# Attention, Fourier mixing and a feed-forward block on one core: a norm's tile, a weight block's step, closing folds, weight scales and a norm behind its halves are moved

## The chip, the cores and the metric

The kernel runs on one core of one Trainium2 chip. The metric is the device time of one execution in microseconds (us), the median of several runs. Five engines work side by side, each through its own queue in order: TensorE (PE: matmuls and transposes, with PEld for its weight loads), VectorE (DVE), ScalarE (ACT), GpSimd (POOL) and SyncE (SP), whose queue issues nearly all DMAs. An instruction waits at the head of its queue until what it needs is there, and everything behind it on that engine waits too.

## The reference, cut to what matters

```
# q, k, v: 8 batches, 12 heads, 448 tokens, 64 per head; w_ch1 768x3072; w_ch2 3072x768
attn = sigmoid(q @ k.T / sqrt(64) - log(448))        # per head, no softmax
x    = heads side by side of attn @ v                # 8 x 448 x 768
u    = x + real(fft(fft(x, axis=tokens), axis=768))  # mixing
un   = (u - mean(u)) / sqrt(var(u) + 1e-6)           # per token
out  = u + relu(un @ w_ch1) @ w_ch2
```

## The kernel before, in words

**Stages.** The 3584 tokens go through three stages: attention with mixing (0 to about 376 us in the profile), the first chunk of 512 tokens through the feed-forward block with plain products (about 384 to 592 us), and six further chunks with a seven-product scheme (to the end). Every matmul that needs more than half precision is made of a high and a low half.

**The step clock of the attention stage.** The loop at line 596 counts a step t from 0 to 202 by twos. Eight steps are one group of four heads (24 groups, 24 steps per batch). In each pass the program writes down scores (lines 139 to 160; ACT takes the sigmoid at line 133), then whatever was registered with `at(t, ...)` for steps t and t+1, then the products with v (line 183; ACT copies them to `xT`, line 192) or, in the third pass of a group, a piece of the mixing of the batch before (`mix_some`). `pin()` chains the instructions of each engine in the order in which they were written down, so an engine's queue order is the program's order.

**What is registered.** (1) `fold` (lines 196 to 217) forms sums and differences of `xT` rows in three levels, ending in the tile `xp`, from which the mixing's matmuls `psd` (line 237) read; the table FOLDS gives step, part and number. All folds are POOL's, except in the last batch, where those at steps after 27 with an odd number are DVE's. (2) `mix_units` (line 227): matmuls `psd`, copies `A` by ACT (line 241), matmuls `pss` (line 247), sums `sm`, `df` by DVE (line 256), transposes `psx` (line 268), sums `u` by DVE (line 277), and stores of `u` to `u_dram`. The tile `u` has four buffers; `psd`, `pss`, `psx` and the products with v share four PSUM banks. (3) `weight(n, step)` (line 308) takes one of 48 blocks of w_ch1 and w_ch2: step 0 loads it into one of four `wr` buffers (SP, line 315), step 1 is ACT's absolute value (line 326), step 2 DVE's maximum (line 331), step 3 three DVE operations that pack it (lines 335 to 340), step 4 its store (SP, line 343). The list `ends` (line 574) has the end step of each block, sorted, and the distances of its five steps from there. A block is named by its end step below: block 90 is the one that ends at step 90. (4) `weight_top`, `weight_row`, `weight_all` and `weight_scales` (lines 345 to 387) turn the 48 maxima into the scales `wsc` through one PE transpose and one small matmul. (5) `norm` (line 429) normalizes the first chunk, four row tiles i of 128 tokens: two loads, statistics, and for each i a cast to a high half by ACT (line 448, n = 8), the low half by DVE (line 452) and two transposing DMAs of the tile `hl` (line 454, n = 9). `hl` has one buffer.

**The first chunk.** `pair` (line 467) makes the feed-forward weights of one block pair: load `wq`, ACT scale (line 482), DVE low half (line 484), four POOL sums (line 492), ACT and DVE once more, store to `w_dram`. The loop at line 835 goes over f: for each f, steps of `pair` around the 18 matmuls of `up_proj` (line 636), then the steps of `fast_norm` that `norm_at` has for this f (the norm of the second chunk, in two halves tp of 18 steps: 0 loads `U`, 1 and 2 statistics, 3 to 6 the inverse root, 8 and 9 scale the rows, 10 to 12 transpose on PE, 13 to 17 sums and halves), then the 24 matmuls of `down_proj` (line 656), then `evac` (line 639), in which ACT and DVE empty the bank `psh` into `hh` and `hl`. `psh` and the transposes `pst` share two banks.

Of the kernel before, what the change touches and what calls it, by code (L numbers as in the profile page):

```python
# [8 lines left out]
F16 = mybir.dt.float16  # L9
F32 = mybir.dt.float32  # L10
# [13 lines left out]
DM = 768  # L24
# [18 lines left out]
NPLAIN = 1  # L43
# [12 lines left out]
def spectral_attention_ffn(tc, qk, v, w1, w2, cd, cs, ident_in, out):  # L56
    nc = tc.nc
    B = qk.shape[0]
# [6 lines left out]
    with ExitStack() as top:  # L65
# [20 lines left out]
        if True:  # L86
            c1 = mix.enter_context(tc.tile_pool(name="c1", bufs=1, side="right"))
            fx = mix.enter_context(tc.tile_pool(name="fx", bufs=1, side="right"))
# [107 lines left out]
            def fold(b, p, n, e):  # L196

                xT, xp, last = xts[b]
                if p == 0 and n == 0:
                    fds[b] = fx.tile([128, 2, 4, HS], F32, tag="fd", name="fd")  # L200
                fd = last if p == 2 else fds[b][:, p]
                lv, n = divmod(n, 2)
                op = (ALU.add, ALU.subtract)[n]
                if lv == 0:
                    if n == 0:
                        eos[p] = fx.tile([128, 2, 2, HS], F32, tag="eo", name="eo")
                    e.tensor_tensor(out=eos[p][:, n], in0=xT[:, p], in1=xT[:, p + 3], op=op)  # L207
                elif lv == 1:
                    eo = eos[p]
                    e.tensor_tensor(out=fd[:, 2 * n:2 * n + 2], in0=eo[:, :, 0], in1=eo[:, :, 1], op=op)  # L210
                elif lv == 2:
                    k = slice(1, 3) if n else slice(0, 4, 3)
                    e.tensor_tensor(out=fd[:, k], in0=fd[:, k], in1=fds[b][:, 1, k], op=op)
                else:
                    fd = fd.rearrange("p (c r) n -> p c r n", c=2)
                    e.tensor_tensor(
                        out=xp[:, n, :, :, 1 - p // 2], in0=fd[:, :, :, 0:HM], in1=fd[:, :, :, HS - 1:HM - 2:-1], op=op)

            def turn_rows(b, back):

                fd, tmp = fds[b], turn[b % 2]
                pairs = ((fd[64:65], tmp[1:3] if back else tmp[0:2]), (fd[0:1, 1:2], tmp[0:1] if back else tmp[2:3]))
                for x, y in pairs:
                    x, y = x.rearrange("o a k n -> o (a k n)"), y.rearrange("(o a) k n -> o (a k n)", o=1)
                    nc.gpsimd.dma_start(*((x, y) if back else (y, x)))
# [165 lines left out]
            def stats(c, j, u):  # L391
                stt = sm.tile([128, 2, 6], F32, tag="st", name="stt")
                for h in range(2):
                    nc.vector.bn_stats(out=stt[:, h], in_=u[:, h * 384:(h + 1) * 384])
                if j == 0:
                    mvs[c] = sm.tile([128, 8, 2], F32, tag="mv", name="mv")
                nc.vector.bn_aggr(out=mvs[c][:, 0:2, j], in_=stt)
# [25 lines left out]
            def scale_rows(c, j, u):  # L423
                mv = mvs[c]
                nc.vector.tensor_scalar(
                    out=u, in0=u, scalar1=mv[:, 0, j:j + 1], scalar2=mv[:, 3, j:j + 1],
                    op0=ALU.subtract, op1=ALU.mult)

            def norm(c, i, n, pool):
                if n == 0:  # L430
                    u = pool.tile([128, DM, 2], F32, tag="un", name="un")
                    u = u.rearrange("p n w -> p (n w)").rearrange("p (i n) -> p i n", i=2)
                    r0 = c * TW + i * 128
                    nc.sync.dma_start(u, u_dram[r0:r0 + 256, :].rearrange("(i p) n -> p i n", p=128))
                    uns[c, i], uns[c, i + 1] = u[:, 0], u[:, 1]
                elif n == 1:
                    stats(c, i % 2, uns[c, i])
                elif n < 6:
                    rsqrt(c, n, nc.vector if n == 2 else nc.gpsimd)
                elif n == 7:  # L440
                    scale_rows(c, i % 2, uns[c, i])
                elif n == 8:
                    u = uns[c, i]
                    if i == 0:
                        ut = ut0.tile([128, 2, NCC * TW], F16, name="ut0")
                        uts[c] = [ut[:, n].rearrange("p (m t) -> p m t", m=NCC) for n in range(2)]
                    hl = fx.tile([128, 2, DM], F16, tag="hl", name="hl")
                    nc.scalar.activation(hl[:, 0], u, AF.Copy)
                    uns[c, i] = u, hl
                else:  # L450
                    u, hl = uns.pop((c, i))
                    nc.vector.tensor_tensor(out=hl[:, 1], in0=u, in1=hl[:, 0], op=ALU.subtract)
                    for n in range(2):
                        nc.sync.dma_start(uts[c][n][:, :, i * 128:(i + 1) * 128], hl[:, n], transpose=True)
# [74 lines left out]
            def pin():  # L529

                ins = nc.cur_bb.bb.instructions
                for i in ins[seen[0]:]:
                    e = str(i.engine)
                    if e in seen[1]:
                        tc.add_manual_dep(
                            i, seen[1][e].name,
                            mybir.DependencyInfo(mybir.DependencyClass.NoSync, mybir.DependencyReason.DATA),
                            reason="order")
                    seen[1][e] = i
                seen[0] = len(ins)  # L540
# [10 lines left out]
            TP = TQ - 12  # L551
            extra = {}

            def at(t, fn):
                extra.setdefault(t, []).append(fn)

            for b in range(B):
                for t, p, n in FOLDS:
                    e = nc.vector if b == B - 1 and t > 27 and n % 2 else nc.gpsimd
                    at(24 * b + t, lambda b=b, p=p, n=n, e=e: fold(b, p, n, e))  # L560
                for k, t in enumerate((22, 25)):
                    at(24 * b + t, lambda b=b, k=k: turn_rows(b, k))
                at(24 * b + 34, lambda b=b: units.extend(mix_units(b)))
            for gg in range(1, GG):
# [3 lines left out]
                for w in range(2):  # L568
                    for n, fn in enumerate((cast, rest)):
# [1 line left out]
            at(17, lambda: nc.sync.dma_start(cd_sb, cd))  # L571
            at(22, lambda: (nc.sync.dma_start(cs_sb, cs), nc.sync.dma_start(ident, ident_in[:, 0]),
                            nc.sync.dma_start(perm, ident_in[:, 1:])))
            ends = sorted([(t, (-10, -5, -1, 0, 3)) for t in range(15, TP, 8)]
                          + [(t, (-11, -3, -1, 0, 3)) for t in range(17, TP, 8)]
                          + [(t, (-10, -2, -1, 0, 3)) for t in (34, 58, 82, 90, 130, 178)])
            for n, (t, ds) in enumerate(ends[:2 * NFC]):
                for step, d in enumerate(ds):
                    at(t + d, lambda n=n, step=step: weight(n, step))
            assert len(ends) >= 2 * NFC  # L580
            at(TP, weight_top)
            at(TP + 4, weight_row)
            at(TP + 6, weight_all)
            at(TP + 6, weight_scales)
            for p, d in ((0, 0), (1, 1)):
                for step, e in enumerate((0, 8 + p, 9 + p)):
                    at(TP + d + e, lambda p=p, step=step: pair(0, p, step))
# [33 lines left out]
        with ExitStack() as fast, ExitStack() as st:  # L621
# [3 lines left out]
            ps_h = fast.enter_context(tc.tile_pool(name="ps_h", bufs=2, space=PSUM))  # L625
# [13 lines left out]
            def evac(c, f):  # L639
                ps = hs[c, f]  # L640
                hh = up.tile([128, TW], F16, tag="hh", name="hh")
                hl = up.tile([128, TW], F16, tag="hl", name="hl")
                nc.scalar.activation(hh, ps, AF.Relu)
                nc.vector.scalar_tensor_tensor(  # L644
                    out=hl, in0=ps, scalar=0.0, in1=hh, op0=ALU.max, op1=ALU.subtract)
                hs[c, f] = (hh, hl)
# [60 lines left out]
            f, m = 1, 0  # L707
# [121 lines left out]

            norm_at = {}  # L830
            for tp in range(2):
                for f, steps in enumerate(((0,), (1,), (2,), (3, 4, 5), (6, 7), (8, 9), (10,), (11,), (12,),
                                           (13, 14), (15, 16), (17,))):
                    norm_at.setdefault(HELD + 1 + 11 * tp + f, []).extend((tp, n) for n in steps)
            for f in range(HELD + 1, NFC + HELD + 1):
                for n in range(2):
                    prepare(2 * f + n)
                    if n == 0 and f < NFC:
                        up_proj(0, f)
                if f in (NFC - 3, NFC - 2):  # L840
                    residual(0, f - NFC + 3)
                for tp, n in norm_at.get(f, ()):
                    fast_norm(NPLAIN, tp, n, ps_h)
                down_proj(0, f - HELD - 1)
                if f < NFC:
                    evac(0, f)
                pin()
                if f in (NFC - 2, NFC):
                    load_w(0, (f - NFC + 2) // 2)
# [209 lines left out]
            for c in range(NPLAIN + 1, NCK):  # L1059
                t = (c - NPLAIN - 1) * NQ * NU  # L1060
# [3 lines left out]
            for g in range(NGR):  # L1064
                t = g * NU
# [121 lines left out]
```

## Time and profile before

| | |
|---|---|
| median of 3 runs | 1583.59 us (1582.77 to 1585.82) |
| the profiled execution's own time | 1585.45 us |
| its span, first to last instruction | 1583.7 us |
| PE busy in the span | 1545.9 us |
| DVE, ACT, POOL busy | 1290.2, 654.5, 357.8 us |

The page gives an engine's busy time and its share of the span. The waits name who stood idle, for what, in total, how often and at longest. A stretch (window) adds the clock that TensorE was granted in it, 1.00 being full speed. A timeline lists instructions in order of time, merged where they follow each other, with the idle time before them and its releaser in brackets.

### The profile page before, as it was taken

The page shows a single profiled execution, that of the slowest core. Times are in us where ns is not written, and L with a number is a line of the kernel's source. Part 1 is how long each engine was busy: PE and PEld are TensorE (multiplying, and loading weights), DVE is VectorE, ACT ScalarE, POOL GpSimd, SP SyncE. Part 2 cuts the span into 40 slices and gives each one's busy share as a digit, 9 for nine tenths or more (in the row PEclk, how much of TensorE's full clock was granted, in tenths as well). Part 3 has the DMA queues.
Part 4 walks back from the last instruction along what each step waited for, and adds up shares of the span by engine and source line. Part 5 has one row for each costly group of instructions (what it writes and reads, how often), then busy time and mean ns, then how long its engine had stood idle before and what let it go on. Part 6 is the DMA issues. An engine that isn't in the chain of part 4 may idle for free.

```text
span 1583.7 us, 27232 instructions
## 1 busy us (share of the span) xinstructions
PE 1545.9 (98%) x10931; PEld 1047.4 (66%) x10931; DVE 1290.2 (81%) x2339; ACT 654.5 (41%) x780; POOL 357.8 (23%) x295
## 2 busy tenths in 40 slices
PE   8999998998999999999999999999999999999998
PEld 3555454554545557777777777777777777777775
DVE  4999897994798956888888888888788878987778
ACT  8777676774545434322232323222423232223221
POOL 2666464675788820000000000000000000000000
PEclk9999999999999999999999999999999999999999
DMA  7888887784778977568657766866676777576571
GB/s 281 313 301 270 331 305 253 297 258 108 261 264 293 323 306 310 189 261 282 232 200 304 232 235 237 293 205 270 257 256 182 279 303 230 163 299 255 201 267 58
DMA packets 131567, 402.42 MB, mean 254 GB/s; under 512 B 69872, under 2 KB 71280, under 8 KB 113008
## 3 DMA queue, kind: packets, MB, share of 16 engines
q1 hardware_dynamic: 130416, 400.50, 70.8%
q8 instruction: 85, 1.39, 0.3%
q0 software_dynamic: 1024, 0.17, 0.1%
q14 instruction: 42, 0.34, 0.1%
HBM read 311.29 MB, written 74.01 MB: 243 GB/s over the span
## 4 chain that ended last, share of the span: by engine, by line
PE 69%; DVE 4%; ACT 1%; DMA 1%; issue 1%; DVEq 0%; ACTq 0%
PE psf L880 30%; PE pso L937 29%; PE psh L636 5%; PE po L656 4%; DVE wp L484 1%; DMA U<-u_dram 1%; DVE F L886 1%; DVE ur L965 0%; DVE H L886 0%; ACT H L915 0%; DVE ur L677 0%; PE psd L237 0%; PE psx L268 0%; DVE acc L1035 0%; DVE acc L952 0%
## 5 line engine op out<-in xcount | busy, mean ns | idle before, releaser
L880 PE MATMUL psf<-ut,ws 128*128 128x256 f16 x4536 | 506.8, 273 | 0.2 <-DVE ur L677 0.2
L937 PE MATMUL pso<-ws,H 128*128 128x384 f16 x3024 | 503.5, 327 | 1.0 <-DVE H L886 0.9
L880 PEld LDWEIGHTS <-ws 128*128 128x128 f16 x4536 | 443.6, 98 | 59.5 <-DVE ur L677 0.4
L937 PEld LDWEIGHTS <-H 128*128 128x128 f16 x3024 | 295.6, 98 | 190.0 <-DVE H L886 1.7
L905 ACT ACTIVATE F<-F 128x1024 f32<-128x1024 f32 x72 | 76.1, 1057 | 406.7 <-DVE F L886 406.7
L952 DVE TENSOR_TENSOR acc<-pso,acc 128x384 f32<-128x384 f32 x399 | 208.0, 551 | 19.9 <-PE pso L937 19.9
L886 DVE TENSOR_TENSOR H<-F,H 128x1024 f16<-128x1024 f32 (+1 forms) x144 | 155.4, 1088 | 48.5 <-ACT H L915 48.3
L133 ACT ACTIVATE a<-sc 128x900 f32<-128x900 f32 x168 | 147.4, 920 | 51.0 <-PE sc L145 49.8
L915 ACT ACTIVATE H<-F 128x1792 f16<-128x1792 f32 x72 | 122.2, 1697 | 110.7 <-DVE F L886 110.7
L886 DVE TENSOR_TENSOR F<-X,psf 128x256 f32<-128x256 f32 x288 | 117.3, 419 | 59.0 <-PE psf L880 54.3
L492 POOL TENSOR_TENSOR wq<-wq 128x384 f32<-128x384 f32 x96 | 148.6, 1553 | 41.5 <-DVE wp L484 35.9
L886 DVE TENSOR_TENSOR F<-F 128x256 f32<-128x256 f32 x288 | 109.5, 422 | 24.8 <-ACT F L905 20.1
L183 PE MATMUL av<-a,vr 128*64 128x450 f32 x576 | 119.1, 550 | 0.0
L484 DVE SCALAR_TENSOR_TENSOR wp<-wq,wsc,wp 128x1536 f16<-128x1536 f32 x48 | 99.0, 2096 | 15.5 <-ACT wp L482 15.5
L886 DVE TENSOR_TENSOR X<-X,psf 128x256 f32<-128x256 f32 x216 | 89.9, 416 | 16.7 <-PE psf L880 14.3
L636 PE MATMUL psh<-ut,wp 128*128 128x512 f16 x432 | 99.8, 384 | 1.8 <-DVE hl L644 1.8
L894 ACT ACTIVATE X<-psf 128x256 f32<-128x256 f32 x72 | 27.8, 386 | 153.7 <-PE psf L880 153.7
L656 PE MATMUL po<-wp,hh 128*128 128x256 f16 (+1 forms) x384 | 88.6, 326 | 0.0
L482 ACT ACTIVATE wp<-wq,wsc 128x1536 f16<-128x1536 f32 x48 | 73.4, 1569 | 28.5 <-DMA wq<-t_dram 23.6
L183 PEld LDWEIGHTS av<-a,vr 128*64 128x64 f32 x576 | 37.2, 136 | 69.2 <-issue 69.1
L207 POOL TENSOR_TENSOR eo<-xT 128x450 f32<-128x450 f32 x47 | 54.0, 1167 | 108.3 <-ACT xT L192 108.0
L636 PEld LDWEIGHTS <-wp 128*128 128x128 f16 x432 | 42.7, 99 | 52.7 <-issue 5.0
(107 smaller groups left out, 1622.5 us busy)
## 6 DMA issues: line engine op xcount, KB each, us to landing
ws<-w_dram SPq DMA_DIRECT2D x144, 1344.0 KB, 8.3
wr<-w_in SPq DMA_DIRECT2D x48, 768.0 KB, 7.9
w_dram<-wp SPq DMA_DIRECT2D x24, 1344.0 KB, 8.2
qk<-qk_in SPq DMA_DIRECT2D x23, 898.0 KB, 7.0
t_dram<-wt SPq DMA_DIRECT2D x48, 384.0 KB, 6.5
wq<-t_dram SPq DMA_DIRECT2D x24, 768.0 KB, 5.7
vr<-v_in SPq DMA_DIRECT2D x24, 448.0 KB, 5.3
U<-u_dram SPq DMA_DIRECT2D x24, 384.0 KB, 9.2
```

What stands on the lines that cost most here:

```text
L133: nc.scalar.activation(a, ps[:, :, :SQ], AF.Sigmoid, bias=-math.log(S), scale=1.0 / math.sqrt(D))
L183: nc.tensor.matmul(ps[j * D:(j + 1) * D, :SQ], vr[:, h:h + D], a[:, j], start=False, stop=(c == 2))
L484: nc.vector.scalar_tensor_tensor(out=w[:, 1, part], in0=t, scalar=sc, in1=w[:, 0, part], op0=ALU.mult, op1=ALU.subtract)
L492: nc.gpsimd.tensor_tensor(out=t[:, o], in0=t[:, x], in1=t[:, y], op=op)
L636: nc.tensor.matmul(hs[c, f], l[:, m], r[:, m], start=(m == n == 0), stop=(m == NCC - 1 and n == 2))
L656: nc.tensor.matmul(po[n][:, at:at + hi - lo], l[:, cols], r[:, lo:hi], start=(f == 0 and m == 0 and at == 0), stop=(f == NFC - 1 and m == ...
L880: nc.tensor.matmul(ps[:, :TH], w[:, x, a, m * 128:(m + 1) * 128], ut[y][:, b, m], start=(m == n == 0), stop=(m == n == 2))
L886: nc.vector.tensor_tensor(out=o, in0=x, in1=y, op=op)
L905: nc.scalar.activation(F[:, 0:4], F[:, 0:4], AF.Relu)
L915: nc.scalar.activation(hts[P][:, 0], F[:, 1:8], AF.Copy)
L937: nc.tensor.matmul(ps[:, :384], H[:, x, a, tp * 128:(tp + 1) * 128], w[:, y, b], start=(j == n == 0 and half != 1), stop=(j == 1 and n == ...
L952: later(0, lambda: nc.vector.tensor_tensor(out=to, in0=ps[:, :384], in1=to, op=ALU.add))
```

## The change

Five edits. In `norm`, tiles i = 1 and 3 take their halves from a buffer of the `u` ring, seen as half precision, and i = 0 and 2 keep the tile `hl`. In the last batch, folds after step 28 (before: 27) with an odd number are DVE's, and every fold after step 28 is written down one step later, at step 198, which puts it behind the piece of mixing at step 196. A weight block ends at step 19 (its load at step 7) and none at step 90; the blocks between take the next lower place in the list. `weight_row` is written down at step 186 instead of 184, `weight_all` and `weight_scales` at 188 instead of 186; `weight_top` stays at 180. In the first chunk, the second chunk's norm has its two statistics steps together, two f after the load, and its steps 1 to 9 stand behind `down_proj` and `evac` of their f; the others stay ahead of `down_proj`.

```
                    if i % 2:
                        hl = fx.tile([128, DM], F32, tag="u", name="u", bufs=4)
                        hl = hl.bitcast(F16).rearrange("p (w n) -> p w n", w=2)
                    else:
                        hl = fx.tile([128, 2, DM], F16, tag="hl", name="hl")
...
-   e = nc.vector if b == B - 1 and t > 27 and n % 2 else nc.gpsimd
-   at(24 * b + t, lambda b=b, p=p, n=n, e=e: fold(b, p, n, e))
+   e = nc.vector if b == B - 1 and t > 28 and n % 2 else nc.gpsimd
+   at(24 * b + t + (b == B - 1 and t > 28), lambda b=b, p=p, n=n, e=e: fold(b, p, n, e))
...
-   ends = sorted([(t, (-10, -5, -1, 0, 3)) for t in range(15, TP, 8)]
+   ends = sorted([(t, (-10, -5, -1, 0, 3)) for t in range(15, TP, 8)] + [(19, (-12, -3, -1, 0, 3))]
                  + [(t, (-11, -3, -1, 0, 3)) for t in range(17, TP, 8)]
-                 + [(t, (-10, -2, -1, 0, 3)) for t in (34, 58, 82, 90, 130, 178)])
+                 + [(t, (-10, -2, -1, 0, 3)) for t in (34, 58, 82, 130, 178)])
...
-   at(TP + 4, weight_row)
-   at(TP + 6, weight_all)
-   at(TP + 6, weight_scales)
+   at(TP + 6, weight_row)
+   at(TP + 8, weight_all)
+   at(TP + 8, weight_scales)
...
-   ((0,), (1,), (2,), (3, 4, 5), (6, 7), (8, 9), (10,), (11,), (12,),
+   ((0,), (), (1, 2), (3, 4, 5), (6, 7), (8, 9), (10,), (11,), (12,),
...
    for tp, n in norm_at.get(f, ()):
-       fast_norm(NPLAIN, tp, n, ps_h)
+       if n > 9 or n == 0:
+           fast_norm(NPLAIN, tp, n, ps_h)
    down_proj(0, f - HELD - 1)
    if f < NFC:
        evac(0, f)
+   for tp, n in norm_at.get(f, ()):
+       if 0 < n < 10:
+           fast_norm(NPLAIN, tp, n, ps_h)
```

## Rows read from the trace of the kernel before

**Rows 1.** The page, part 1: busy us (share of the span) xinstructions of each engine.
```profile
PE 1545.9 (98%) x10931; PEld 1047.4 (66%) x10931; DVE 1290.2 (81%) x2339; ACT 654.5 (41%) x780; POOL 357.8 (23%) x295
```
**Rows 2.** Waits of PE, whole span: us in total, times, longest us.
```profile
PE pss L247 <- ACT A L241: 6.1, 2, 5.8
PE psx L268 <- DVE u L277: 5.4, 1, 5.4
...
PE psx L268 <- ACT A L241: 3.4, 2, 2.3
PE psx L268 <- DVE df L256: 3.0, 6, 0.5
PE psh L636 <- DVE hl L644: 1.8, 1, 1.8
PE pswt L353 <- DVE df L256: 1.7, 1, 1.7
PE pst L760 <- DVE hl L644: 1.6, 1, 1.6
```
**Rows 3.** Windows: stretch length, busy us per engine (xinstructions), granted clock, DMA share, GB/s.
```profile
173.20:179.90 6.70, 6.62 (x33) 3.31 (x33) 5.65 (x9) 3.91 (x6) 3.04 (x5) 0.51 1.01 372
256.20:262.10 5.90, 5.80 (x18) 3.46 (x18) 2.05 (x4) 1.57 (x4) 1.36 (x2) 0.53 1.00 340
...
382.90:390.20 7.30, 7.17 (x25) 3.42 (x26) 2.93 (x7) 0.00 (x0) 6.91 (x8) 0.65 0.45 142
...
60.00:340.00 280.00, 265.84 (x1711) 150.72 (x1709) 246.70 (x333) 202.22 (x271) 162.69 (x155) 0.98 0.83 292
```
**Rows 4.** Timeline of SP: start us, us, engine line, operation, out<-in xcount.
```profile
29.49 0.33 SPq L343 DMA_DIRECT2D t_dram<-wt  x1
...
155.05 0.35 SPq L315 DMA_DIRECT2D wr<-w_in  x1
...
158.89 5.36 SPq L315 DMA_DIRECT2D wr<-w_in  x2
...
255.21 1.43 SPq L315 DMA_DIRECT2D wr<-w_in  x2
```
**Rows 5.** Line 315 (weight loads): landing after issue.
```profile
DMA to landing us min/median/max: 4.7/7.9/11.9
```
**Rows 6.** Timeline of ACT in the attention stage; in brackets idle before and releaser.
```profile
29.19 0.55 ACT L192 ACTIVATE xT<-av 128x450 f32<-128x450 f32 x1 [0.18 <-PE av L183]
...
38.81 0.96 ACT L326 ACTIVATE wt<-wr 128x768 f32<-128x768 f32 x1
...
169.04 0.91 ACT L326 ACTIVATE wt<-wr 128x768 f32<-128x768 f32 x1 [5.27 <-DMA wr<-w_in]
...
252.12 0.84 ACT L448 ACTIVATE hl<-un 128x768 f16<-128x768 f32 x1 [6.62 <-DMA ut<-hl]
...
268.81 0.95 ACT L326 ACTIVATE wt<-wr 128x768 f32<-128x768 f32 x1
```
**Rows 7.** Timeline 363 to 397 of POOL, PE and ACT, around the closing folds.
```profile
363.34 1.92 POOL L207 TENSOR_TENSOR eo<-xT 128x450 f32<-128x450 f32 x2 [12.98 <-ACT xT L192]
...
377.36 1.40 POOL L210 TENSOR_TENSOR xp<-eo 128x450 f32<-128x450 f32 x1 [0.65 <-PE psx L268]
...
383.35 8.39 POOL L492 TENSOR_TENSOR wq<-wq 128x384 f32<-128x384 f32 x8
...
390.18 2.18 PE L237 MATMUL psd<-cd_sb,xp 128*113 128x198 f32 x12
...
395.59 0.92 PE L247 MATMUL pss<-A,cs_sb 113*113 113x396 f32 x2 [0.26 <-ACT A L241]
...
392.12 3.03 ACT L482 ACTIVATE wp<-wq,wsc 128x1536 f16<-128x1536 f32 x2
```
**Rows 8.** Timeline 436 to 467 of DVE, the first chunk's first norm half.
```profile
436.46 1.02 DVE L394 BATCH_NORM_STATS2 stt<-U 128x6 f32<-128x384 f32 x2 [7.11 <-DMA U<-u_dram]
...
464.09 2.62 DVE L425 TENSOR_SCALAR U<-U,mv 128x768 f32<-128x768 f32 x2
```

More of the change, by code (lines that the diff above doesn't have):

```diff
@@ L446, in norm @@
                         uts[c] = [ut[:, n].rearrange("p (m t) -> p m t", m=NCC) for n in range(2)]
-                    hl = fx.tile([128, 2, DM], F16, tag="hl", name="hl")
+                    if i % 2:
+                        hl = fx.tile([128, DM], F32, tag="u", name="u", bufs=4)
+                        hl = hl.bitcast(F16).rearrange("p (w n) -> p w n", w=2)
+                    else:
+                        hl = fx.tile([128, 2, DM], F16, tag="hl", name="hl")
                     nc.scalar.activation(hl[:, 0], u, AF.Copy)
@@ L831, in spectral_attention_ffn @@
             for tp in range(2):
-                for f, steps in enumerate(((0,), (1,), (2,), (3, 4, 5), (6, 7), (8, 9), (10,), (11,), (12,),
+                for f, steps in enumerate(((0,), (), (1, 2), (3, 4, 5), (6, 7), (8, 9), (10,), (11,), (12,),
                                            (13, 14), (15, 16), (17,))):
```

## The prediction, made before the changed kernel was run

> **What bounds the kernel now.** First the page: PE is busy 1545.9 us of a span of 1583.7 [rows 1], so all idle time of PE together is 38 us, and a change that leaves the matmuls alone can win only from that, and from matmuls that ran at a low clock. Next the waits of PE [rows 2]: they name few places. `pss` stood 5.8 us for a copy `A` of ACT; `psx` 5.4 us for a sum `u` of DVE, 3.4 us (two waits) for `A`, and six times about 0.5 us for `df`; `psh` 1.8, `pswt` 1.7 and `pst` 1.6 us, all for DVE. Then the windows at these places [rows 3]: behind the three longest, PE was granted 0.51, 0.53 and 0.65 of full speed, so each long wait is paid again, by length times the missing share: 6.70 x 0.49 = 3.3, 5.90 x 0.47 = 2.8 and 7.30 x 0.35 = 2.6 us. All lies before 470 us. Last the timelines, for what each releaser had itself waited for: ACT for a weight load (5.27) and for the transposing DMAs of `hl` (6.62) [rows 6], DVE for `U` (7.11) [rows 8].
>
> **The change, part by part** (gains in us).
>
> *Block 90 goes.* ACT's absolute value for block 95 stood until 169.04 for its load, which SP issued at 158.89, behind the store of block 82 and the load of block 90 at 155.05 [rows 4, 6]. The store of 82 still stands ahead, so the issue stays near 158.9, but the data now share the DMA engines with one load of 768 KB less. Such loads land 4.7 us after issue at best and 7.9 at the median [rows 5], so at 163.6 to 166.8; I take 165. PE's 3.4 us of waits [rows 2] then shrink to some 0.7 (ACT still has sigmoids and a cast ahead of `A`), too little to be followed by 3.3 us of low clock. Gain 3.4 - 0.7 + 3.3 = 6.0; bounds 2.2 (landing at the median, clock low all the same) and 6.7.
>
> *Block 19 comes.* It adds one ACT operation of 0.96 (as at 38.81) to a stretch in which ACT idles only some 0.2 us between pieces (0.18 at 29.19) [rows 6]. With it, blocks 15 to 23 fill the four `wr` buffers, so block 25's load now waits in SP for block 15, whose packing is done when its store leaves at 29.49 [rows 4]; landing is 37.4 at the median of rows 5, ahead of its use at 38.81, and 41.4 at the slowest, 11.9. From block 39 on, every block waits for the same predecessor as before. DVE's extra four operations lie in its idle time. Taken: -0.6; bounds -3.5 (0.96 and 2.6 of a late load) and 0.
>
> *Row tiles 1 and 3 leave `hl`.* The cast at 252.12 no longer waits 6.62 [rows 6], so `pss` no longer stands 5.8 [rows 2] and the 2.8 of low clock go: 8.6 at stake. The next thing late is block 143's load, issued at 255.21 in a queue that the cast does not move [rows 4]; it lands at 260.3 to 263.5, while ACT now comes to it 8.4 earlier than 268.81 [rows 6], at 260.4. A wait of up to 3.1 on ACT, of which PE feels the part over about 1.9 (5.27 on ACT gave 3.4 on PE above): I take 1.1. Gain 7.5; bounds 0.7 (the slowest landing, and a low clock again) and 8.6.
>
> *Scales later.* `pswt` no longer catches DVE before `weight_top`: 1.7 [rows 2]. But `weight_scales` now stands in the same step as the first ACT scaling that reads `wsc`, ahead of the copies that free banks for `psx`. I give back half: 0.9; bounds -1.7 (the wait only moves there) and 1.7.
>
> *Closing folds.* At step 196 DVE ran its share of the last folds ahead of the mixing's sums, so `psx` stood 5.4 [rows 2], and 2.6 of low clock followed: 8.0 at stake. Now DVE goes to the sums at once. But POOL does all four folds of step 196 alone, from 375.7 (377.36 less the idle 0.65 and one operation of 0.98) [rows 7]. A fold costs POOL 0.96 with DVE idle and up to 1.40 beside it [rows 7]; at 1.2 the four end at 380.5, three more at 1.3 at 384.4 (before: 383.35). PE, 8.0 earlier, wants `psd` at 382.2 and gets its first operand at about 383.5. Behind the folds POOL forms four weight sums at 8.39/8 = 1.05 each [rows 7], to 388.6; ACT's scaling behind them (half of 3.03) ends at 390.1, the copy behind it at 390.6, and there `pss`, before at 395.59, starts [rows 7]. Gain 4.9, with two short waits of 1.3 and 1.9 on the way (1.7 and 1.8 were followed by no low clock). Bounds 8.0, and -0.1: with every POOL operation at 1.40 the copy ends at 393.1, and a low clock takes 2.6.
>
> The Trainium skill ("GPSIMD Engine Reference", key points) says that POOL shares its SBUF interfaces with DVE, and contends with DVE instructions that have two SBUF inputs or run in a two-port mode. DVE's sums here read one input from PSUM, so by that rule the four folds would run at rows 7's 0.96 and this part would gain 5.9. The same page says that DVE is about twice as fast for such work, which speaks against giving POOL two folds more; by the rows that price is already in the chain.
>
> *Norm behind its halves.* The statistics waited 7.11 for `U` [rows 8] with the `hl` of f = 5 behind them on DVE, and `psh` of f = 7 stood 1.8 [rows 2]. Now that `hl` stands ahead, and `U` has landed when the statistics come; this wait goes whole. `pst`'s 1.6 goes only in part: `pst` needs the scaled rows, and scaling (2.62 from 464.09 [rows 8]) now stands behind an `hl`; only what DVE has caught up helps. I take 0.9 of it. Gain 2.7; bounds 1.1 (`pst` 0.7 later, the length of that `hl`) and 3.4. Below nothing is excluded, since DVE's order no longer puts `hl` behind a DMA.
>
> *Denser DVE.* Between 60 and 340 us DVE is busy 246.7 of 280, 88% [rows 3]; with 13.5 us of that stretch gone and one block (some 3.5) less it is 91%. The waits for `df`, 3.0 in six places [rows 2], should grow: -2.0; bounds -3 and 0.
>
> **Sum.** 6.0 - 0.6 + 7.5 + 0.9 + 4.9 + 2.7 - 2.0 = 19.4. The profiled execution took 1585.45, so 1566.0; the median of the runs is 1.86 below that execution, so 1564.2. All bounds at their best give 28.4 (1555.2), all at their worst -4.3 (1587.9).
>
> **Rivals.**
> 1. *The waits come back on DVE.* What holds PE in the attention stage would be DVE's 88%, and ACT's stalls only gave it time. For it: the `df` waits. Against it: DVE itself stood idle over 6 us while `pss` waited. Then the load and the cast win only their lower part: 2.2 + 3.0 (half the idle) - 0.6 + 0 + 2.5 + 1.1 = 8.2, so 1575.4.
> 2. *The change does not free the cast.* A buffer of `u` may still be held by a sum whose store is behind SP's queue when the cast comes, so ACT stands as long as before. Against it: four buffers, and the oldest of four sums was stored a group earlier. The 7.5 are missing: 1571.7.
> 3. *Every gap closes* and nothing new opens: 1555.2.
> 4. *Slower: the early block.* In the first 60 us ACT passes every delay on to PE. If each block's load behind block 19 came late by block 25's worst, 2.6, eight blocks in a row would cost 21 and outweigh all gains; from there on the change loses. With ten, 1564.2 + 26 - 0.6 = 1589.6. Against it: the shift of predecessors ends after blocks 25, 31, 33 and 34, so the delay should stop at four.
>
> **How the numbers follow.** The forecast (gains of 13 to 26) 0.66; rival 1 0.15; rival 2 0.08; rival 3 0.06; rival 4 0.05. About 0.2% (3.2 us) is what a measurement of this kernel can tell from no change. Rival 1 has a tail of 0.05 that ends within that. So faster 0.90, same 0.05, slower 0.05. The range goes from just above rival 3 to just past rival 1: 1556 to 1577, leaving out about 0.15.
>
> **What would show it.** Right: `pss` waits for `A` no longer near 6 us, ACT's cast waits for no `hl`; the load wait near 169 halved; the clock at 1.00 in the stretches that were at 0.51 and 0.53; `psx` waits for `u` gone and instead `psd` or `pss` for POOL's folds or `A` by 1 to 2 us each; `psh` for `hl` gone, `pst` reduced. PE's idle time should fall from 38 to about 25. Wrong: a wait of ACT over 4 us for the load behind block 130's group, a low clock behind the closing folds, block 25 late at 39 us, or waits of PE on DVE over 5 us in sum.

## The result

The changed kernel takes 1568.93 us (median of 4 runs, 1567.79 to 1570.26); the kernel before, run beside it on the same chip, 1583.18 us (4 runs, 1580.05 to 1585.82). The ratio is 0.9911, 95% interval 0.9891 to 0.9932: faster, by 14.3 us of the medians. The forecast was 1564.2, with a range of 1556 to 1577. The profiled execution of the changed kernel took 1567.79 us with a span of 1566.0, against 1585.45 and 1583.7: 17.7 us less, where the sum said 19.4. Line numbers above 447 of the kernel before are four to eight higher in the changed one (the cast of line 448 is now at 452, the packing of 484 at 488, `hl` of 644 at 648, `pst` of 760 at 764).

First the page, part 1, of the changed kernel (as [rows 1]):

```profile
PE 1539.5 (98%) x10931; PEld 1044.0 (67%) x10931; DVE 1295.2 (83%) x2337; ACT 653.9 (42%) x780; POOL 371.4 (24%) x297
```

PE has as many matmuls as before in 6.4 us less (fewer of them ran at a low clock), and 26.5 us of idle time where it had 38.

The waits of PE in the changed kernel (us in total, times, longest us; as [rows 2]):

```profile
PE psx L268 <- ACT A L241: 4.3, 3, 2.3
...
PE sc L145 <- DVE lo L129: 2.7, 4, 1.0
PE psx L268 <- DVE df L256: 2.7, 6, 0.5
...
PE pss L247 <- ACT A L241: 1.8, 1, 1.8
PE psd L237 <- DVE xp L216: 1.2, 1, 1.2
```

`pss` for `A` fell from 6.1 to 1.8, `psx` for `u` from 5.4 to 0.7 (not shown), and `psh`, `pswt` and `pst` are gone. But `psx` for `A`, which was to shrink from 3.4 to 0.7, grew to 4.3, and `lo` went from 1.2 to 2.7.

Windows of the changed kernel (stretch length, busy us per engine, granted clock, DMA share, GB/s; as [rows 3]):

```profile
60.00:340.00 280.00, 271.27 (x1766) 154.52 (x1765) 258.04 (x335) 209.44 (x280) 177.29 (x161) 0.99 0.84 296
160.00:180.00 20.00, 19.20 (x127) 10.45 (x123) 19.27 (x28) 14.52 (x20) 6.81 (x6) 1.00 0.90 329
...
263.20:268.20 5.00, 4.39 (x27) 2.64 (x31) 3.70 (x6) 3.27 (x6) 2.81 (x4) 0.66 1.02 420
...
381.20:390.20 9.00, 8.96 (x47) 6.44 (x48) 6.72 (x9) 2.96 (x6) 5.50 (x6) 1.00 0.68 230
```

Two of the three low stretches of [rows 3] are at full speed now, 2.4 GHz: the one near 173 (0.51) and the one behind the closing folds (0.65). The third has moved: it is at 263 to 268, at 0.66, a mix of 1.2 and 2.4 GHz. DVE is busy 92% of the attention stage (258.04 of 280).

Where the 17.7 us came from is read off landmarks, the starts of the same matmul in both timelines (us; group k is the four heads that begin at step 8k):

| landmark of PE | before | after | gained since the line above | predicted |
|---|---|---|---|---|
| half-scores of group 5 (line 158) | 66.53 | 67.10 | -0.57 | -0.6 |
| group 16 | 238.66 | 232.68 | 6.55 | 6.0 |
| group 23 | 353.12 | 344.01 | 3.13 | 7.5 |
| first `pss` behind group 23 | 374.99 | 365.41 | 0.47 | 0.9 |
| first `pss` behind the folds | 395.59 | 381.24 | 4.77 | 4.9 |
| end of the span | 1583.7 | 1566.0 | 3.35 | 2.7 |
| denser DVE, inside these stretches | | | | -2.0 |

One term is far off, and it is the largest: the cast. Within its stretch, group 16 to 17 took 24.27 us before and 16.20 after, 8.07 gained; group 17 to 18 took 14.33 before and 19.24 after, 4.91 given back. The timelines of the changed kernel (start us, us, engine, line, operation, in brackets idle before and releaser) show it engine by engine. ACT, as [rows 6]:

```profile
166.01 0.92 ACT L326 ACTIVATE wt<-wr 128x768 f32<-128x768 f32 x1 [2.36 <-DMA wr<-w_in]
...
239.39 0.86 ACT L452 ACTIVATE u<-un 128x768 f16<-128x768 f32 x1
...
259.54 0.93 ACT L326 ACTIVATE wt<-wr 128x768 f32<-128x768 f32 x1 [4.58 <-DMA wr<-w_in]
```

The cast at 239.39 waits for nothing, the load wait of 5.27 is down to 2.36, and block 143's load is waited for 4.58 us at 259.54. SP, as [rows 4]:

```profile
228.06 11.90 SPq L315 DMA_DIRECT2D wr<-w_in  x2
...
250.87 1.50 SPq L315 DMA_DIRECT2D wr<-w_in  x2
```

Block 143's load is the first of the pair at 250.87; the data came 8.7 us later, in a stretch in which the DMA engines were full (share 1.04 from 240 to 260). PE:

```profile
257.95 0.37 PE L145 MATMUL sc<-hi,lo 64*128 64x450 f32 x2
...
263.81 0.59 PE L268 MATMUL psx<-perm,xT 128*113 128x128 f32 x3 [2.26 <-ACT A L241]
...
264.98 0.58 PE L145 MATMUL sc<-hi,lo 64*128 64x450 f32 x2
...
374.23 2.24 PE L237 MATMUL psd<-cd_sb,xp 128*113 128x198 f32 x12 [1.23 <-DVE xp L216]
...
381.24 0.92 PE L247 MATMUL pss<-A,cs_sb 113*113 113x396 f32 x2 [1.79 <-ACT A L241]
...
449.26 0.60 PE L764 MATMUL pst<-ident,U 128*128 128x128 f32 x4
```

ACT's delay becomes PE's 2.26 us at 263.81, and behind it the same pair of score matmuls takes 0.58 in place of 0.37: half speed. That is 2.26, and 5.0 x 0.34 = 1.7 for the stretch at 0.66, 4.0 of the 4.91.

### The profile page after: what moved, and what is told of

The parts are those of the page before. It is cut to its first block, busy times and chain, and to the rows that moved or that the text cites. A ratio compares the mean times of both kernels' runs of the same rounds, so it can differ in the third digit from the quotient of the medians.

```text
span 1566.0 us, 27233 instructions
## 1 busy us (share of the span) xinstructions
PE 1539.5 (98%) x10931; PEld 1044.0 (67%) x10931; DVE 1295.2 (83%) x2337; ACT 653.9 (42%) x780; POOL 371.4 (24%) x297
## 4 chain that ended last, share of the span: by engine, by line
PE 70%; DVE 3%; DMA 2%; ACT 1%; issue 0%; POOL 0%; DVEq 0%; POOLq 0%; ACTq 0%
PE psf L888 29%; PE pso L945 29%; PE po L660 6%; PE psh L640 6%; DMA ws<-w_dram 2%; DVE F L894 1%; DVE ur L973 0%; DVE H L894 0%; ACT H L923 0%; DVE ur L681 0%; POOL wq L496 0%; DVE acc L1043 0%; DVE acc L960 0%; ACT F L913 0%; DVE X L894 0%
## 5 line engine op out<-in xcount | busy, mean ns | idle before, releaser
L496 POOL TENSOR_TENSOR wq<-wq 128x384 f32<-128x384 f32 x96 | 152.9, 1599 | 27.4 <-DVE wp L488 21.7
```

The costliest lines, as they stand in the source:

```text
L496: nc.gpsimd.tensor_tensor(out=t[:, o], in0=t[:, x], in1=t[:, y], op=op)
```

## The experiments

Each is the changed kernel with the edit shown; times are medians, ratios are to the kernel before on the same chip. "Span" is that of the profiled execution, to be held against 1566.0. The runs are on several chips, and executions of one kernel differ by up to 7.4 us (1564.74 to 1572.17, with the block at 106). Group 5 alone starts between 67.1 and 69.1 us in kernels that are equal up to there. A difference of some 2 us between two spans therefore shows nothing by itself; the stretch in which an edit acts says more.

**The cast goes back to one buffer.**

```
-                    if i % 2:
-                        hl = fx.tile([128, DM], F32, tag="u", name="u", bufs=4)
-                        hl = hl.bitcast(F16).rearrange("p (w n) -> p w n", w=2)
-                    else:
-                        hl = fx.tile([128, 2, DM], F16, tag="hl", name="hl")
+                    hl = fx.tile([128, 2, DM], F16, tag="hl", name="hl")
```

> All edits but the row tiles' buffer. Theory (the cast's 8 us are won and then mostly given back, because block 143's load stands behind the group of blocks 127, 129, 130 in SP's queue): the cast waits 6 to 7 us for hl again, pss stands near 6 us, and the load of block 143 is no longer waited for; the end is only 2.5 to 4 us later than the changed kernel (span near 1569). Rival (the edit is worth its full 8 us, and the later load wait comes from the blocks' new order): 7 to 9 us later (span near 1574), with the load wait still there.

1572.37 us, ratio 0.9936 (0.9921 to 0.9951), span 1570.7. The waits of ACT in its attention stage:

```profile
ACT wt L326 <- DMA wr<-w_in: 8.3, 5, 3.2
ACT hl L448 <- DMA ut<-hl: 6.3, 1, 6.3
```

The 6.30 is back, and no load is waited for near 260. From group 16 to 23 it takes 113.93 us, against 111.33 in the changed kernel: there the edit is worth 2.6, about what the landmarks gave (3.13). The span is 4.7 longer, past the theory's 2.5 to 4, but 1.75 of that had come by group 16, ahead of the edit; the wait of `pss` is 4.85, not near 6. Either the cast's stall was never worth 7.5, or the load takes back what it wins; this run doesn't tell which.

**The blocks go back** (90 in the list, none at 19).

```
-    ... [(19, (-12, -3, -1, 0, 3))] ... (34, 58, 82, 130, 178)
+    ...                             ... (34, 58, 82, 90, 130, 178)
```

> All edits but the weight blocks: block 90 back, none at step 19. Theory: the wait of ACT near 169 us is again about 5 us, PE's clock low behind it, span 4.5 to 6 us longer (near 1571). Rival (with the other edits in, PE is later limited by DVE anyway, so the stall is absorbed): under 2 us longer.

1570.85 us, 0.9923 (0.9905 to 0.994), span 1570.1. The load wait is back on ACT's timeline:

```profile
169.19 0.91 ACT L326 ACTIVATE wt<-wr 128x768 f32<-128x768 f32 x1 [5.22 <-DMA wr<-w_in]
```

Group 11 to 12 takes 20.95 in place of 15.67, so 5.28 is lost there, of the 6.55 in the table. But at group 23 only 2.95 is left: group 16 to 23 runs in 108.87 in place of 111.33. The load of block 143 is still waited for (4.73 on ACT, 2.25 on PE); most of the difference, 1.46, lies in group 17 to 18, where this time no low clock followed PE's wait (see the last section). The mechanism is the theory's; of the sizes, the span's 4.1 lies just under its 4.5 to 6, and the medians are 1.9 apart, as in the rival.

**Block 130 ends at 154, at 106, at 13.** Three places for the one extra block that stands ahead of block 143.

```
-    ... (34, 58, 82, 130, 178)
+    ... (34, 58, 82, 154, 178)      # second: 106 for 154
+    ... (34, 58, 82, 178), and (13, (-12, -2, -1, 0, 3))      # third
```

> The changed kernel with the extra block of step 130 at step 154. Theory: block 143 now waits for block 127's buffer, its load leaves SP some 4 to 8 us earlier, ACT waits under 1 us for it, psx's 2.3 us and the low clock at 264 to 268 us go; span 3 to 5 us shorter (near 1562), less what a group 151, 153, 154 costs (up to 1). Rival (DVE is what holds PE there): PE waits on lo or df instead, span within 1 us of the changed kernel.

> The same with step 106 in place of 154. Theory: the wait near 260 us goes as with 154; a group 103, 105, 106 costs what 79, 81, 82 costs now, 0.8 us of PE; span 3 to 4.5 us shorter than the changed kernel. Rival (DVE): within 1 us.

> The changed kernel with the extra block of step 130 at step 13, where DVE is idle about 8 us. Theory (the wait near 260 us is the group's, and what 154 and 106 lost again was the price of a new group in a dense place): no load wait near 260, no new group later; the early stretch costs 0.5 to 1.5 us; span 3 to 4.5 us shorter than the changed kernel (near 1562). Rival (ACT has no room in the first 60 us, each operation there costs its 0.9 and a late load more): 2 us or more are lost early and the gain is under 2.

At 154: 1565.64, 0.9894 (0.9879 to 0.9909), span 1565.1. At 106: 1569.01, 0.9913 (0.989 to 0.9935), span 1567.7. At 13: 1565.44, 0.9902 (0.9885 to 0.992), span 1566.0. In all three the load wait near 260 is gone and group 17 to 18 takes 14.33, the 4.9 us won whole. By the spans 4.0, 6.6 and 4.9 us are lost elsewhere. By the ratios, which allow for the chip, the kernels are 2.7 us faster, 0.3 slower and 1.4 faster than the changed one, and all intervals overlap with its own, so the net gain stays open. Some of the loss stands where the block now is: at 106, group 14 to 15 went from 14.34 to 16.91; at 154, group 20 to 21 from 14.33 to 16.06; at 13, group 4 starts at 53.16 in place of 49.16, with PE waiting 1.80 for DVE's `lo` at 42.88, the clock at 0.66 from 42 to 46 us, and behind both a late load:

```profile
48.49 0.91 ACT L326 ACTIVATE wt<-wr 128x768 f32<-128x768 f32 x1 [2.66 <-DMA wr<-w_in]
```

So a block was not free at any of the three places, and moving it confounds the wait that it takes away with the work that it adds. The last is my slower rival at its mild size. How the 4 us at group 4 divide between ACT's 2.66, DVE and the clock, this run does not tell.

**The closing folds go back.**

```
-   e = nc.vector if b == B - 1 and t > 28 and n % 2 else nc.gpsimd
-   at(24 * b + t + (b == B - 1 and t > 28), ...)
+   e = nc.vector if b == B - 1 and t > 27 and n % 2 else nc.gpsimd
+   at(24 * b + t, ...)
```

> All edits but the closing folds. Theory (worth about 5 us, since the 5.4 us wait and its low clock give way to two waits of 1.2 and 1.8 us on the folds' chain): psx stands 5 to 6 us for u, clock low in the 7 us behind it, span 4 to 6 us longer (near 1571). Rival (the wait was cover for the chain POOL, ACT, PE, which ends when it ends): under 2 us longer.

1572.32 us, 0.9941 (0.9923 to 0.996), span 1571.7, of which 3.94 us lies behind group 23 (1225.93 against 1221.99 to the end). Its waits of PE, and a window in which the changed kernel has 18.97 us of PE at 1.00:

```profile
PE psx L268 <- DVE u L277: 5.4, 1, 5.4
```

```profile
370.00:392.00 22.00, 16.63 (x77) 10.99 (x78) 10.07 (x16) 5.81 (x8) 12.51 (x12) 0.84 0.26 70
```

The 5.4 us wait and the low clock return together. The folds are worth 3.9 by this run, 4.8 by the landmarks, 4.9 by the sum; the other 1.8 of the span's 5.7 had come by group 23.

**The norm goes back ahead of its halves** (the table of steps and the place of steps 1 to 9, as before the change).

> All edits but the place of the second chunk's norm. Theory: the statistics again wait about 7 us for U, psh stands 1.5 to 2 and pst 1.5 to 2 us, no low clock; span 3 to 4 us longer (near 1569.5). Rival (DVE's other waits in the stretch leave it enough slack, now that PE comes to the chunk earlier): under 1 us.

1569.71 us, 0.9923 (0.9907 to 0.994), span 1568.2; from group 23 to the end 1.66 us more. The timeline of DVE, and that of PE:

```profile
420.13 1.02 DVE L394 BATCH_NORM_STATS2 stt<-U 128x6 f32<-128x384 f32 x2 [4.59 <-DMA U<-u_dram]
```

```profile
451.70 0.66 PE L764 MATMUL pst<-ident,U 128*128 128x128 f32 x4 [1.85 <-DVE hl L648]
```

The wait for `U` is 4.59 in place of [rows 8]'s 7.11: DVE comes to it 13.8 us earlier (415.54 against 429.35), but the load is issued 14.9 earlier (409.85 against 424.75) and its data are there 10.3 us later in place of 11.7. And `psh` no longer waits at all: with the other edits in, there was only `pst`'s 1.9 left to win. That lies between the theory (3 to 4) and the rival (under 1).

**The later scaling.** The kernel with block 130 at 13, and in the first chunk's plan the second ACT and DVE scaling of the first weight pair (steps 4 and 5) at place 3 in place of 2, which is three fills (sixths of an `up_proj`) later.

```
+   k = 3 if (i, p) == (0, 0) and step in (4, 5) else max(4 * p + d + 6 * i, min(step, 2))
```

> The kernel with the block at step 13, and the second ACT and DVE scaling of the first weight pair three fills later. Theory (pss's 1.8 us stand for a copy queued behind an ACT scaling that waits for POOL): that wait goes, span 1.5 to 2 us shorter than with the block alone. Rival (another copy or PSUM bank is just as late): under 0.5.

1563.33 us, 0.9889 (0.9873 to 0.9905), span 1563.2, so 2.8 less than with block 130 at 13 alone. `pss` no longer waits 1.8 for `A`: ACT's scaling, which stood 1.42 us in the changed kernel for POOL's weight sums, is no longer ahead of that copy. That is the theory, but not all of the 2.8 is the wait: in the profiled execution with block 130 at 13 alone, the clock behind it was at 0.76 for 7 us, which is 1.7 us, and in the changed kernel it was not.

**Block 143's load three steps earlier,** which takes the load wait away and adds no work. (The expectations of this and the next runs say three groups, and mean three steps t: 13 ahead of the block's end in place of 10.)

```
-    ends = sorted([(t, (-10, ...
+    ends = sorted([(t, (-13 if t == 143 else -10, ...
```

> The changed kernel with one thing moved: block 143's load of the mixing weights is issued three groups earlier (13 steps ahead of its conversion in place of 10). My theory: the 4.58 us in which ScalarE waited for that load at 259.5 us were what gave back the cast's gain, through the 2.26 us gap of TensorE at 263.8 and the lower clock behind it. With the load landed by then, ScalarE's wait is under 1 us, that gap is gone, groups 17 to 18 stand about 14.3 us apart in place of 19.2, and the span is 1561 to 1563 us (3 to 5 less than 1566.0). Rival (as the two runs with block 130 moved showed, which lost elsewhere 3.6 to 6 us of the 4.9 won here): the end of the attention is set by VectorE's and ScalarE's total work, and other waits take the place of this one; the span is 1565 to 1567.

1566.61 us (1563.97 to 1568.98), 0.9902 (0.9885 to 0.9919); the profiled execution is the fastest of its runs, span 1562.2. SP issues the load at 246.59, 4.3 us earlier; ACT has it in time, and PE's gap is gone (timelines of SP, of ACT and of PE):

```profile
246.59 0.59 SPq L315 DMA_DIRECT2D wr<-w_in  x1
```

```profile
254.43 0.95 ACT L326 ACTIVATE wt<-wr 128x768 f32<-128x768 f32 x1
```

```profile
260.24 1.14 PE L268 MATMUL psx<-perm,xT 128*113 128x128 f32 x9
...
261.83 0.37 PE L145 MATMUL sc<-hi,lo 64*128 64x450 f32 x2
```

The scores behind it run at full speed (0.37). Group 17 to 18 takes 15.1 in place of 19.24, and at group 23 PE is 3.4 us earlier. Part is lost again in the next group, 16.15 in place of 14.97: ACT now waits 1.64 for a later load, at 271.61. In the medians the gain is 2.3 us, within the spread of either kernel's runs, so the profile carries this one.

**Two loads earlier, and those of all regular blocks from 23 on,** each with the later scaling.

```
+    (-13 if t in (95, 143) else -10, ...      # first
+    (-13 if t > 15 else -10, ...              # second
```

> The changed kernel with the loads of blocks 95 and 143 three groups earlier, and the first scaling of the first inverse's two steps three groups later (the one edit which in the run with block 130 at step 13 took 2.8 us off by ending the wait of the half-products for ScalarE's A, 1.8 us). Theory: both gains add up, 3 to 5 us from the load of block 143 and 1.5 to 3 from the later scaling, block 95's load (ScalarE waited 2.36 us for it at 166 us) under 1 us: span 1558 to 1562. Rival: the later scaling is worth nothing once the attention ends at another time: span like that of the run with block 143's load alone, within 1 us.

> As the run with the loads of blocks 95 and 143 and the later scaling, but every regular block from 23 on has its load three groups earlier. Theory: only the loads that ScalarE waited for in the changed kernel (6 waits, 12.8 us in all, the longest 4.58 and 2.36 us) can win, so this is within 1 us of the run before, 1558 to 1562. Rival: the loads issued earlier stand ahead of the attention's own loads and stores in SyncE's queue and wait there for their buffers (11.1 us for one at 228 us), so that some group comes late; 1564 or more.

Two loads: 1562.73 us, 0.9878 (0.9864 to 0.9893), span 1562.1. The waits for blocks 95 and 143 are gone, but ACT stood 1.51 us for a later load at 272.98, where the changed kernel had no wait. It also stood 3.15 at 122, and group 8 to 9 took 16.4 in place of 14.4. That is not the edit's, since both loads are issued behind it: the wait near 120 is 1.41 to 2.67 in the runs whose kernels are equal up to there. By the spans (1562.1 against 1562.2 with block 143's load alone) the rival holds, by the medians (3.9 us less) the theory; from group 23 to the end 1.4 us are won, so the later scaling is worth something, and how much stays open. All loads: 1560.20 us (1560.05 to 1560.38), 0.9862 (0.9846 to 0.9879), span 1558.3. ACT's six waits for loads, 12.8 us in the changed kernel, are all gone. No group came late for SP's queue, so the rival falls. Of the theory the time holds, the "within 1 us" of the run with two loads doesn't: there 9.2 us of load waits were left on ACT, and ending them was worth another 2.5. This is the fastest kernel of the study, 8.7 us below the changed one by the medians (7.8 by the ratios, whose intervals do not touch), 21.8 below the one before. Its runs lie within 0.33 us of each other, those of the changed kernel within 2.5.

**All loads earlier, and the cast back to one buffer.** The test of the cast's term where no load can take it back.

> The run with all loads of the weight blocks earlier and the later scaling, with one thing taken back: every half of the norm goes through the one buffer again, as before the change. It tells whether my 7.5 us for the freed conversion were wrong in themselves or were given back by block 143's load. In the run with the buffers split, groups 16 to 23 take 106.4 us, against 111.3 in the changed kernel. Theory: where no load is waited for the conversion's wait (about 6.3 us on ScalarE) comes back whole, groups 16 to 23 take 112 to 114.5 us, and the span is 1558.3 + 5.5 to 8, so 1564 to 1566. Rival: the conversion was worth only the 2.6 to 3.2 us that it made in the changed kernel, and the earlier loads are worth the rest by themselves: groups 16 to 23 take 109 to 110 us, span 1561 to 1562.

1566.72 us (1566.39 to 1567.29), 0.9908 (0.9891 to 0.9924), span 1564.8. ACT and PE (timelines), and the window behind:

```profile
244.76 0.84 ACT L448 ACTIVATE hl<-un 128x768 f16<-128x768 f32 x1 [6.74 <-DMA ut<-hl]
```

```profile
248.94 1.66 PE L247 MATMUL pss<-A,cs_sb 113*113 113x396 f32 x2 [5.92 <-ACT A L241]
```

```profile
245.00:255.00 10.00, 6.06 (x30) 3.36 (x34) 3.59 (x6) 6.12 (x10) 3.90 (x4) 0.66 0.99 346
```

The stall comes back as it was before the change (5.92 on PE, then a low clock). Groups 16 to 23 take 113.35 us, against 106.44 with the buffers split: the cast is worth 6.9 there, 6.5 in the span and 6.5 in the medians. In the changed kernel the same edit was worth 2.6. The theory holds, the rival (109 to 110) falls.

## Why the prediction was right, and the term that was not

**Block 90 and block 19.** Together 5.4 was predicted, 5.98 had come by group 16, in part by chance. At the place of the load wait, groups 11 to 13, 5.59 came (36.23 us before, 30.64 after), and with the blocks back 5.30 are lost there. Another 1.26 came at group 8 to 9 (15.68 to 14.42) and is not the edit's, since the run with the blocks back takes 14.33. Nor is the 0.57 at group 5 shown to be the early block's: it is within the spread of that landmark, and without block 19 group 5 started at 68.18. The 3.4 us of waits of PE in the sum was right by coincidence. One of the two waits for `A` lies elsewhere, at 124.69, and near 170 PE also stood for `xT`, which the sum did not have (1.15, and 2.26 for `A`, make 3.41; the timeline of PE in the kernel before):

```profile
124.69 0.59 PE L268 MATMUL psx<-perm,xT 128*113 128x128 f32 x3 [1.11 <-ACT A L241]
...
170.43 0.59 PE L268 MATMUL psx<-perm,xT 128*113 128x128 f32 x3 [1.15 <-ACT xT L192]
```

Eight blocks late in a row, the slower rival, did not come: ACT's load waits there are 0.97 and 2.35, at 44 and 58 (0.52 and 1.04 in the kernel before), and 1.17 at 74; the fourth comes only at 120.

**The cast: 7.5 predicted, 3.1 measured.** This is the mis-sized term. The mechanism was right: no wait for `hl`, no `pss` for `A`, no low clock behind it. The next thing late was named too, block 143's load. Its size was wrong. From SP's issue to ACT being ready I had 5.2 us (255.21 to 260.4), with landing 5.1 to 8.3 after issue, so a wait of up to 3.1, of which PE felt 1.1, and no low clock. There were 4.1 us (250.87 to 254.96, which is 259.54 less 4.58), since the gains up to there had moved ACT by 13.9 and SP's issue by only 4.3, and landing took 8.7. So ACT waited 4.58, PE 2.26, and then PE ran at half speed for a stretch, as behind the 5.27 near 169 in the kernel before. That half speed was not bound to come: in the run with the norm undone, equal in this stretch, it did not, and groups 16 to 23 took 110.19 in place of 111.33. The run with that load earlier won 3.4 at group 23, and the pair with all loads earlier shows the term at 6.9: nearly all of the 7.5 was there, and was handed to the next wait.

**Scales.** 0.9 predicted, 0.47 came. `pswt` waits no longer, and ACT now waits 1.52 for `wsc`, which is the half given back that the step named.

**Closing folds.** 4.9 predicted, 4.77 came, by the path described: `psd` waits 1.23 (1.3 predicted), `pss` 1.79 (1.9), no low clock. The last was luck in part. In the runs with block 130 at 106 and at 13 the same `pss` stood 1.80 and 1.79, and the clock fell, where the changed kernel has 1.00 from 381.20 to 390.20. The window of 7 us behind the wait at 106:

```profile
381.46:388.46 7.00, 7.00 (x31) 5.47 (x32) 3.57 (x5) 1.34 (x3) 3.38 (x2) 0.76 0.59 178
```

The inner steps differ from the sum's. POOL and DVE in the changed kernel, timelines around the folds:

```profile
366.15 1.92 POOL L207 TENSOR_TENSOR eo<-xT 128x450 f32<-128x450 f32 x2 [4.81 <-ACT xT L192]
368.15 1.92 POOL L210 TENSOR_TENSOR xp<-eo 128x450 f32<-128x450 f32 x2
371.12 1.46 POOL L213 TENSOR_TENSOR xp<-xp,fd 128x450 f32<-128x450 f32 x1 [1.06 <-DVE xp L213]
372.54 1.06 POOL L216 TENSOR_TENSOR xp<-fd 128x452 f32<-128x452 f32 x1
373.67 1.33 POOL L216 TENSOR_TENSOR xp<-xp 128x452 f32<-128x452 f32 x1
```

```profile
369.03 1.01 DVE L277 TENSOR_TENSOR u<-psx,sm 112x384 f32<-112x384 f32 x2
...
370.96 0.62 DVE L216 TENSOR_TENSOR xp<-fd 128x452 f32<-128x452 f32 x1
372.61 1.47 DVE L216 TENSOR_TENSOR xp<-xp 128x452 f32<-128x452 f32 x1 [1.03 <-POOL xp L213]
...
423.88 1.00 DVE L394 BATCH_NORM_STATS2 stt<-U 128x6 f32<-128x384 f32 x2
```

The four folds took 0.96 each beside DVE's sums from PSUM, where I had put 1.2; then POOL stood 1.06 us for DVE's fold, which the sum had not, and ended at 374.96 (374.8 by my steps, less the 9.6 gained ahead). Two errors of 1 us cancelled. The Trainium skill ("GPSIMD Engine Reference", key points) has POOL contend with DVE instructions with two SBUF inputs; this trace agrees: `eo<-xT` took POOL 0.96 beside DVE's sums from PSUM, and 1.62 at 121.48 beside DVE's packing of weights, with two SBUF inputs (POOL and DVE of the changed kernel):

```profile
121.48 3.25 POOL L207 TENSOR_TENSOR eo<-xT 128x450 f32<-128x450 f32 x2 [10.73 <-ACT xT L192]
```

```profile
122.27 1.62 DVE L340 SCALAR_TENSOR_TENSOR wt<-wr,wt 128x768 int32<-128x768 int32 x1
```

In the closing folds themselves it is not shown: POOL's `xp<-fd` took 1.06 beside DVE's fold, and 1.06 at 59.22 with no fold of DVE beside it. By that rule the part was to gain 5.9; it did not, because of the wait for DVE.

**Norm behind its halves.** 2.7 predicted, 3.35 from the folds to the end; the statistics at 423.88 wait for nothing, and `pst` at 449.26 neither, where I had left 0.7 of a wait. Undone alone it costs 1.66. The two differ because what stood in its place in the kernel before depended on when `U` landed, and the other edits had already moved that.

**Denser DVE.** The waits for `df` did not grow (3.0 to 2.7), those for `lo` did, by 1.5: 1.2 in all, against 2.0. They lie inside the stretches of the table. DVE was busy 92% there, 91% predicted, and did not take the gains back as the first rival has it.

**The sum against the runs.** 17.7 came of 19.4 in the profiled executions. The other 3 us of the miss of 4.7 in the median are the last line of the sum: the profiled execution of before lay 1.86 above the median of its runs, and I carried that over; that of after lies 1.14 below its own. Two of the signs named for being wrong appeared. ACT waited over 4 us for the load behind block 130's group, and that is the mis-sized cast. PE waited 8.4 us for DVE in sum, over the 5 named; that sign told little, since the sum was 15.8 in the kernel before. Block 25 was in time at 38.62, and no low clock stood behind the closing folds.

## What to carry to other kernels

A stall that is taken away hands its time to the next wait in the same queue, and that one has to be sized with every gain ahead of it, not with the one edit's. Price an edit together with its cover: the same two buffers were worth 2.6 us where the load behind the cast was late, and 6.9 where it was issued three steps earlier. Where a queue's loads stand just in time, moving the one that was waited for left a wait of 1.5 and 1.6 us at a later one in the two runs that did so; moving all of them early, as their buffers allow, took away six waits at no cost that any view showed. And before a gain is put down to an edit, look at whether it lies where the edit acts, and whether the run with the edit undone loses it there.

## What the runs showed of the hardware

How a gap of PE and its clock went together: the gap's length alone did not decide it. Behind 1.59 (two loads earlier, at 126.6) and 1.85 us the next matmuls ran at full speed; behind 4.85 to 5.92 us a stretch at half speed followed each time. Between these the same gap went both ways. Behind 1.79 to 1.81 us the clock stayed in most runs and fell in those with block 130 at 106 and at 13. Behind the 2.26 us near 264 it fell in the changed kernel and with the folds undone; with the norm undone it stayed, as behind 2.25 with the blocks back. Two of these, from kernels that are equal up to there (folds undone, then norm undone; PE, and the window of 5 us from the end of the gap):

```profile
265.69 0.59 PE L268 MATMUL psx<-perm,xT 128*113 128x128 f32 x3 [2.26 <-ACT A L241]
```

```profile
265.69:270.69 5.00, 5.00 (x31) 2.83 (x31) 4.27 (x7) 3.12 (x5) 2.21 (x4) 0.66 1.04 433
```

```profile
265.94 0.59 PE L268 MATMUL psx<-perm,xT 128*113 128x128 f32 x3 [2.26 <-ACT A L241]
```

```profile
265.94:270.94 5.00, 5.00 (x39) 2.59 (x41) 4.27 (x7) 3.83 (x6) 2.22 (x4) 1.00 1.04 433
```

Group 17 to 18 took 19.50 us in the first and 18.05 in the second. So the low clock behind a wait of some 2 us is a price that may or may not be paid, and a forecast should carry it as a range; what decides it stays open here.

Near 60 us, too, a gap of 1.99 to 2.16 us comes in some executions, with half speed behind it each time. The 2.16 is from the run with the norm undone, its timeline of PE and its window:

```profile
59.96 0.65 PE L145 MATMUL sc<-lo,hi 64*128 64x450 f32 x2 [2.16 <-DVE lo L129]
```

```profile
60.00:62.00 2.00, 2.00 (x7) 1.42 (x8) 1.93 (x4) 0.92 (x2) 1.92 (x2) 0.52 0.86 310
```

In the profiled execution of the changed kernel that gap is 0.97 us, and the window is at 1.00. It came, at 1.99 to 2.16 us, in five runs whose kernels have nothing changed before 60 us but, in one, loads: cast, folds and norm undone, two loads earlier, all loads earlier. Group 5 started at 68.1 to 69.1 us in them, against 67.1. One microsecond more of that wait thus goes with a start of group 5 that is 1 to 2 us later, and two executions may differ by it; why it comes in one and not in the other was not tried. In the fastest kernel it is still there, 2.15 of the 2.6 us that PE waits for `lo`.
